# A matmul step with 96 instead of 128 weight columns, and issued one step earlier

## The chip, the cores and the metric

The kernel runs on one core of a Trainium2 chip. The metric is the device time of one execution in microseconds (us), as the median of several runs. Of the core's engines, TensorE (PE) does the matmuls, with the weight loads shown as a row of their own (PEld); VectorE (DVE) and ScalarE (ACT) do the elementwise work, SyncE (SP) issues most of the transfers.

## The reference

Three layers follow each other on 4 x 4096 = 16384 tokens of 192 channels: a causal convolution with 7 taps per head, a gated layer of 1536 hidden units, and a squared-relu layer of 2048 hidden units.

```python
out = np.einsum('hk,bskhg->bshg', w, x_unf)          # w: softmax over the 7 taps
...
gate = 1.0 / (1.0 + np.exp(-(x @ w_gate)))
val = x @ w_val
return (gate * val @ w_out).astype(np.float32)       # first layer
...
h = x @ w_in
r = np.maximum(h, 0.0)
g = r * r
return (g @ w_out).astype(np.float32)                # second layer
```

All is float32 in and out.

## The kernel before

Channels lie on partitions, tokens along the free dimension, in 32 tiles of 512 tokens. A tile goes through the gated layer (kind 1, 12 units of 128 hidden units each) and, three tiles later, through the squared-relu layer (kind 2, 8 units of 2 x 128). A unit is the work of `rows` (the matmuls into the hidden units, line 427), `activate` (ScalarE and VectorE, lines 444 to 456) and `cols` (the matmuls back to the 192 channels, line 479). PE works through them in the order in which the last loop writes them: the `rows` of a unit, then the `cols` of a unit before it.

The matmuls run on float32r operands, which hold fewer bits than float32. So each operand is split in a high and a low part, and each product is made of steps: high x high, high x low, low x high. The product of two low parts isn't needed. In `activate`, `gh` (line 455, ScalarE) is the high part of a hidden block of 128 units x 512 tokens, and `gl` (line 456, VectorE) the rest. Both have five buffers.

Every matmul uses 64 of the array's 128 rows, and each step is a pair of them, one for each half of the rows (`HALVES`). The two halves sum up in banks of their own, `sums[0]` and `sums[1]`, which `fold` adds (lines 490 to 498).

The 192 output channels make two blocks. Block a has 128 channels and the bank `accA`. Block b has 64, so its weights `wb` hold two things in their 128 columns: the 64 columns of the high part of the weights, and then the 64 columns of the low part. One step with `gh` over all 128 columns so gives high x high and low x high at once; the bank `accB` has the two on its partitions 0 to 63 and 64 to 127, and `fold` adds the one to the other (lines 497 and 498). The step with `gl` gives high x low on partitions 0 to 63, and low x low on 64 to 127.

So `cols` makes five steps (ten matmuls) for each hidden block: on accA high x gh, high x gl and low x gh, on accB all x gh and all x gl. The first step into a bank starts its sum (`start`), and the last one ends it (`stop`); start and stop are set for places 0 and 3, and 2 and 4, of the list of steps. There are 32 x 12 + 32 x 8 x 2 = 896 hidden blocks.

Weights are loaded into the array by an instruction of their own ahead of each matmul; the text of the kernel has one call for both.

Of the kernel before, what the change touches and what calls it, by code (L numbers as in the profile page):

```python
# [17 lines left out]
HB = 64  # L18
NT = 512
BLK = 32  # L20
# [4 lines left out]
def kernel(  # L25
# [356 lines left out]
    def prep_x(t, a_on_array=False, b_on_array=False):  # L382


        p, i = divmod(t, 2)
        j = p % TPB
        sa, a = convolve("A", i, lambda: xin.pop(t), j, a_on_array)
        b = []
        if i == 0:
            pairs[p], b = convolve("B", 0, lambda: xin.pop(("B", p)), j, b_on_array)  # L390

        def over():
            done(sa)
            if i == 1:
                done(pairs.pop(p))

        return a, b, part_ops(t, x1, "x1", lambda: sa["cv"], lambda: pairs[p]["cv"], over)
# [63 lines left out]
    def cols(u):  # L461

        key = (u.kind, u.t)
        if u.f == 0:
            acc[key] = [[banks.take(f"acc{nm}") for nm in "AB"] for _ in HALVES]
        sums = acc[key]
        for i, v in enumerate(u.hidden):
            if u.kind == 1:  # L470
                w, lo = w1[:, u.f, NR:], N1 + HB
            else:
                w, lo = wo2[:, 2 * u.f + i, :], NO + HB
            wa, wb, wl = w[:, 0:P], w[:, P : 2 * P], w[:, lo : lo + P]
            steps = ((0, wa, v.gh), (0, wa, v.gl), (0, wl, v.gh), (1, wb, v.gh), (1, wb, v.gl))
            first, last = u.f == 0 and i == 0, u.last and i == len(u.hidden) - 1
            for k, (b, wt, m) in enumerate(steps):
                for h, half in enumerate(HALVES):
                    nc.tensor.matmul(  # L479
                        sums[h][b][1], wt[half], m[half],  # L480
                        start=(first and k in (0, 3)), stop=(last and k in (2, 4)),
                    )
        return u.last
# [83 lines left out]
    with tc.manual_schedule():  # L567
# [59 lines left out]
        for t in range(2, NTILE):  # L627
            at = where[1, t, 0]
            before = starts[starts.index(at) - 1]
            a, b, parting = prep_x(t)  # L630
# [17 lines left out]
        for e, u in enumerate(units):  # L648
            rows(u)
            activate(u)  # L650
            for o in stores:
                o()
            stores = []
            k = e - max(s for s in starts if s <= e)
            due = len(pending) if k == 0 else 0 if k == 1 else len(pending) - 1
            for _ in range(due):
                v = pending.popleft()
                if cols(v):
                    stores += (evac1 if v.kind == 1 else evac2)(v.t)
            pending.append(u)  # L660
            for o in side[e]:
                o()
        while pending:
            v = pending.popleft()
            if cols(v):
                for o in evac2(v.t):
                    o()
# [39 lines left out]
```

## Time and profile before

| | |
|---|---|
| median of 3 runs | 2454.08 us (2453.99 to 2456.96) |
| profiled execution | 2455.46 us, its span 2453.6 us |
| PE busy | 2395.8 us (98%), 20512 matmuls |
| PEld busy | 1936.4 us (79%), 20512 loads |
| DVE busy | 1704.9 us (69%) |
| ACT busy | 1308.5 us (53%) |

The span reaches from the first to the last instruction of the profiled execution. A busy share says how much of the span an engine had something recorded as running. For PE this isn't the same as working at its peak: matmuls overlap in the array, and the profile models where they end. What can be read well is when they start.

### The profile page before, as it was taken

How to read it: one execution, taken by the hardware profiler on the slowest of the kernel's cores; microseconds unless marked ns; L12 is line 12 of the kernel's file. 1: busy time of each engine (PE TensorE's matmuls, PEld its weight loads, DVE VectorE, ACT ScalarE, POOL GpSimd, SP SyncE). 2: the span in 40 equal slices, each digit the busy share in tenths (PEclk: the TensorE clock that was granted, in tenths of full speed). 3: DMA queues.
4: the chain of work that ended last, by engine and by line, in shares of the span. 5: the costliest groups of instructions: out<-in, count | busy, mean ns of one | idle time of the engine just before them, and what ended most of it. 6: DMA issues, size and time to landing. Idle time of an engine off the chain costs nothing.

```text
span 2453.6 us, 49309 instructions
## 1 busy us (share of the span) xinstructions
PE 2395.8 (98%) x20512; PEld 1936.4 (79%) x20512; DVE 1704.9 (69%) x2676; ACT 1308.5 (53%) x2260; POOL 24.8 (1%) x97
## 2 busy tenths in 40 slices
PE   6898999999999999999999999999999999999998
PEld 3576888888888888888888888888888888888886
DVE  5776767676776766767676776766767676776676
ACT  5555555554555554555554555554555554555564
POOL 1000000000000000000000000000000000000000
PEclk8999999999999999999999999999999999999999
DMA  6232111112111121211112111121211112111111
GB/s 126 65 78 57 40 23 31 33 34 42 38 21 35 29 38 38 40 23 31 33 34 42 38 20 36 29 38 38 41 22 31 34 33 42 38 21 27 25 35 27
DMA packets 226896, 92.12 MB, mean 38 GB/s; under 512 B 202857, under 2 KB 214257, under 8 KB 226673
## 3 DMA queue, kind: packets, MB, share of 16 engines
q1 hardware_dynamic: 226272, 88.39, 17.8%
q8 instruction: 160, 2.62, 0.4%
q0 software_dynamic: 256, 0.52, 0.1%
q14 instruction: 64, 0.52, 0.1%
q10 hardware_dynamic: 144, 0.07, 0.0%
HBM read 26.03 MB, written 12.58 MB: 16 GB/s over the span
## 4 chain that ended last, share of the span: by engine, by line
PE 91%; DVE 4%; ACT 2%; issue 1%; DMA 1%; SPq 0%; DVEq 0%; ACTq 0%
PE pg L427 29%; PE accA L479 24%; PE ph L427 22%; PE accB L479 16%; DVE s L445 1%; ACT gh L455 1%; PE pv L427 1%; DVE gl L456 1%; DVE cvA L328 0%; DMA raw<-in_moe_w_out_dram 0%; ACT s L444 0%; DMA x<-x 0%; PE cv L337 0%; DVE cvB L328 0%; DVE w L168 0%
## 5 line engine op out<-in xcount | busy, mean ns | idle before, releaser
L427 PE MATMUL pg<-x,w 64*128 64x512 f32 x3456 | 866.3, 393 | 26.5 <-ACT w L157 22.4
L427 PE MATMUL pv<-x,w 64*128 64x512 f32 x3456 | 863.1, 393 | 14.2 <-DMA x<-x 10.3
L455 ACT CAST gh<-s 128x512 fp32r<-128x512 f32 x896 | 555.6, 621 | 520.0 <-DVE s L445 401.6
L456 DVE TENSOR_TENSOR gl<-s,gh 128x512 fp32r<-128x512 f32 x896 | 608.0, 692 | 286.2 <-ACT gh L455 264.0
L427 PEld LDWEIGHTS pg<-x,w 64*128 64x128 f32 x3456 | 639.3, 186 | 168.4 <-ACT w L157 27.1
L427 PEld LDWEIGHTS pv<-x,w 64*128 64x128 f32 x3456 | 639.7, 186 | 31.6 <-DVE s L445 11.6
L427 PE MATMUL ph<-x,wr 64*128 64x512 f32 x4608 | 573.4, 391 | 0.0
L427 PEld LDWEIGHTS ph<-x,wr 64*128 64x128 f32 x4608 | 431.9, 184 | 103.1 <-DVE s L445 0.4
L448 DVE TENSOR_TENSOR s<-s 128x512 f32<-128x512 f32 x512 | 330.3, 686 | 150.6 <-ACT s L447 149.7
L479 PE MATMUL accA<-gh,wo 64*128 64x512 f32 x2048 | 402.8, 390 | 0.0
L447 ACT ACTIVATE s<-ph 128x512 f32<-128x512 f32 x512 | 277.5, 594 | 214.6 <-PE ph L427 213.9
L445 DVE TENSOR_TENSOR s<-pv,s 128x512 f32<-128x512 f32 x384 | 263.2, 685 | 184.5 <-ACT s L444 184.0
L444 ACT ACTIVATE s<-pg 128x512 f32<-128x512 f32 x384 | 228.1, 594 | 245.5 <-PE pv L427 238.0
L479 PE MATMUL accA<-gh,w 64*128 64x512 f32 x1536 | 312.0, 390 | 0.0
L479 PEld LDWEIGHTS accA<-gh,wo 64*128 64x128 f32 x2048 | 192.3, 184 | 44.4
L479 PE MATMUL accA<-gl,wo 64*128 64x512 f32 x1024 | 200.4, 388 | 0.0
L479 PE MATMUL accB<-gh,wo 64*128 64x512 f32 x1024 | 200.4, 388 | 0.0
L479 PE MATMUL accB<-gl,wo 64*128 64x512 f32 x1024 | 199.9, 387 | 0.0
L479 PEld LDWEIGHTS accA<-gh,w 64*128 64x128 f32 x1536 | 157.5, 185 | 31.6 <-ACT gh L455 0.2
L479 PE MATMUL accA<-gl,w 64*128 64x512 f32 x768 | 158.5, 389 | 0.2 <-DVE gl L456 0.2
L479 PE MATMUL accB<-gh,w 64*128 64x512 f32 x768 | 158.0, 388 | 0.0
L479 PE MATMUL accB<-gl,w 64*128 64x512 f32 x768 | 157.9, 388 | 0.0
(92 smaller groups left out, 1442.4 us busy)
## 6 DMA issues: line engine op xcount, KB each, us to landing
x<-x SPq DMA_DIRECT2D x192, 256.0 KB, 3.8
out_dram<-oA SPq DMA_DIRECT2D x128, 64.0 KB, 2.0
xiA<-in_x_dram SPq DMA_DIRECT2D x124, 64.0 KB, 3.6
out_dram<-oB SPq DMA_DIRECT2D x64, 64.0 KB, 2.0
xiB<-in_x_dram SPq DMA_DIRECT2D x60, 64.0 KB, 2.8
rawr<-in_moe_w_in_dram SPq DMA_DIRECT2D x16, 192.0 KB, 3.4
rawo<-in_moe_w_out_dram SPq DMA_DIRECT2D x16, 192.0 KB, 2.5
raw<-in_moe_w_gate_dram SPq DMA_DIRECT2D x12, 192.0 KB, 3.3
```

Source lines behind the costliest of these rows:

```text
L427: nc.tensor.matmul(u.banks[h][1], w[half, o + c * P : o + (c + 1) * P], xs[1][half, place[c][h] + p, :], start=(i == 0), stop=(i == len(st ...
L444: nc.scalar.activation(s, u.banks[0][1], AF.Sigmoid)
L445: nc.vector.tensor_tensor(s, u.banks[1][1], s, op=ALU.mult)
L447: nc.scalar.activation(s, u.banks[i][1], AF.Relu)
L448: nc.vector.tensor_tensor(s, s, s, op=ALU.mult)
L455: nc.scalar.copy(v.gh, s)
L456: nc.vector.tensor_tensor(v.gl, s, v.gh.bitcast(F32), op=ALU.subtract)
L479: nc.tensor.matmul(sums[h][b][1], wt[half], m[half], start=(first and k in (0, 3)), stop=(last and k in (2, 4)),)
```

## The change

The step with gl on accB takes the first 96 (`HB + BLK`) columns of `wb` in place of all 128, and writes partitions 0 to 95 of accB. It leaves out the last 32 columns of low x low. It also changes places with the step with gh on accB, so that gl comes fourth and gh fifth. The first hidden block of each tile and layer, where accB starts its sum, keeps the old order, with gl last.

```diff
-            steps = ((0, wa, v.gh), (0, wa, v.gl), (0, wl, v.gh), (1, wb, v.gh), (1, wb, v.gl))
+
+
+            steps = [
+                (0, wa, v.gh), (0, wa, v.gl), (0, wl, v.gh), (1, wb[:, 0 : HB + BLK], v.gl), (1, wb, v.gh),
+            ]
             first, last = u.f == 0 and i == 0, u.last and i == len(u.hidden) - 1
+            if first:
+                steps[3:] = steps[:2:-1]
             for k, (b, wt, m) in enumerate(steps):
                 for h, half in enumerate(HALVES):
                     nc.tensor.matmul(
-                        sums[h][b][1], wt[half], m[half],
+                        sums[h][b][1][0 : wt.shape[1]], wt[half], m[half],
                         start=(first and k in (0, 3)), stop=(last and k in (2, 4)),
                     )
```

PE's rows for an ordinary hidden block, the second one of the first tile, stand as follows in the program before (-) and in the changed one (+); the last number is partitions x columns that a matmul writes, x2 the two halves, and `w` the weights w1.

```order
 L427 MATMUL pv<-x_179,w_70 128x512
-L479 MATMUL accA<-gh,w_70 128x512 x2
-L479 MATMUL accA<-gl,w_70 128x512 x2
-L479 MATMUL accA<-gh,w_70 128x512 x2
-L479 MATMUL accB<-gh,w_70 128x512 x2
-L479 MATMUL accB<-gl,w_70 128x512 x2
+L485 MATMUL accA<-gh,w_70 128x512 x2
+L485 MATMUL accA<-gl,w_70 128x512 x2
+L485 MATMUL accA<-gh,w_70 128x512 x2
+L485 MATMUL accB<-gl,w_70 96x512 x2
+L485 MATMUL accB<-gh,w_70 128x512 x2
 L427 MATMUL pg<-x_179,w_70 128x512
```

The two steps on accB have changed places, and the one with gl is 96 wide; 832 of the 896 blocks look like this.

At the first hidden block of the first tile, PE's rows are these.

```order
-L479 MATMUL accB<-gh,w_70 128x512 x2
-L479 MATMUL accB<-gl,w_70 128x512 x2
+L485 MATMUL accB<-gh,w_70 128x512 x2
+L485 MATMUL accB<-gl,w_70 96x512 x2
 L427 MATMUL pg<-x_179,w_70 128x512
```

Here only the width differs, as in the other 63 blocks that start a sum. No other row of PE, and no row of another engine, has moved.

## Rows read from the trace of the kernel before

**Rows 1.** The page's first part: busy time, share and instructions of PE and others.
```profile
PE 2395.8 (98%) x20512; PEld 1936.4 (79%) x20512; DVE 1704.9 (69%) x2676; ACT 1308.5 (53%) x2260; POOL 24.8 (1%) x97
```

**Rows 2.** The page's chain of work that ended last, by line.
```profile
PE pg L427 29%; PE accA L479 24%; PE ph L427 22%; PE accB L479 16%; DVE s L445 1%; ACT gh L455 1%; PE pv L427 1%; DVE gl L456 1%; DVE cvA L328 0%; DMA raw<-in_moe_w_out_dram 0%; ACT s L444 0%; DMA x<-x 0%; PE cv L337 0%; DVE cvB L328 0%; DVE w L168 0%
```

**Rows 3.** Three stretches: length, busy us (instructions) by engine, clock, DMA.
```profile
core 0: us, PE busy (x) PEld busy (x) DVE busy (x) ACT busy (x) POOL busy (x), PEclk, DMA share, GB/s
196.00:200.00 4.00, 4.00 (x22) 3.39 (x20) 1.24 (x4) 0.60 (x1) 0.19 (x1) 0.50 0.31 98
...
300.00:1300.00 1000.00, 1000.00 (x8698) 815.58 (x8696) 702.77 (x1074) 533.09 (x921) 8.14 (x35) 1.00 0.17 33
1300.00:2300.00 1000.00, 1000.00 (x8700) 815.72 (x8698) 690.75 (x1052) 527.34 (x910) 7.88 (x34) 1.00 0.17 33
```

**Rows 4.** Timeline from 1200 us: start, length (us), engine, line, instruction.
```profile
1201.07 0.39 PE L479 MATMUL accB<-gh,w 64*128 64x512 f32 x2
1201.07 0.19 PEld L479 LDWEIGHTS accB<-gl,w 64*128 64x128 f32 x2
...
1201.30 0.39 PE L479 MATMUL accB<-gl,w 64*128 64x512 f32 x2
1201.30 0.19 PEld L479 LDWEIGHTS accA<-gh,w 64*128 64x128 f32 x2
1201.52 0.39 PE L479 MATMUL accA<-gh,w 64*128 64x512 f32 x2
```

**Rows 5.** Timeline of PE from 196 us, one half's matmuls four pairs apart.
```profile
196.39 0.63 PE L427 MATMUL pv<-x,w 64*128 64x512 f32 x1
...
198.10 0.63 PE L427 MATMUL pv<-x,w 64*128 64x512 f32 x1
```

**Rows 6.** The page's costliest groups: busy us, mean ns | idle before.
```profile
L479 PE MATMUL accB<-gl,wo 64*128 64x512 f32 x1024 | 199.9, 387 | 0.0
...
L479 PE MATMUL accB<-gl,w 64*128 64x512 f32 x768 | 157.9, 388 | 0.0
```

**Rows 7.** Timeline of PEld from 31.8 us, loads of one half after a pause.
```profile
31.89 0.18 PEld L427 LDWEIGHTS pg<-x,w 64*128 64x128 f32 x1 [0.76 <-issue]
...
32.00 0.19 PEld L427 LDWEIGHTS pg<-x,w 64*128 64x128 f32 x1
```

**Rows 8.** Timeline from 167.7 us, around loads that waited for VectorE.
```profile
167.83 0.62 PE L479 MATMUL accB<-gl,w 64*128 64x512 f32 x2
...
168.06 0.39 PE L427 MATMUL pg<-x,w 64*128 64x512 f32 x1
...
168.26 0.18 PEld L427 LDWEIGHTS pv<-x,w 64*128 64x128 f32 x1 [0.25 <-DVE s L445]
...
168.29 0.47 PE L427 MATMUL pv<-x,w 64*128 64x512 f32 x1
...
168.37 0.19 PEld L427 LDWEIGHTS pv<-x,w 64*128 64x128 f32 x1
...
168.60 0.39 PE L427 MATMUL pv<-x,w 64*128 64x512 f32 x1
```

**Rows 9.** ACT's waits for line 455: us in total, times, longest us.
```profile
ACT gh L455 <- DVE s L445: 401.6, 384, 3.7
...
ACT gh L455 <- DVE s L448: 111.7, 258, 1.6
```

**Rows 10.** Timeline of PE, the last 128-row matmuls ahead of 64-row ones.
```profile
30.94 1.02 PE L337 MATMUL cv<-xTA,diag 128*128 128x512 f32 x2
...
31.37 0.59 PE L337 MATMUL cv<-xTA,diag 128*128 128x512 f32 x1
```

**Rows 11.** Timeline of PEld, two stretches: float32 loads (L337), float32r loads (L427).
```profile
8.95 0.29 PEld L337 LDWEIGHTS cv<-xTB,diag 128*128 128x128 f32 x1 [3.40 <-ACT diag L302]
...
9.11 0.34 PEld L337 LDWEIGHTS cv<-xTB,diag 128*128 128x128 f32 x1
...
60.77 0.28 PEld L427 LDWEIGHTS pg<-x,w 64*128 64x128 f32 x1 [0.95 <-DVE w L168]
...
60.94 0.33 PEld L427 LDWEIGHTS pg<-x,w 64*128 64x128 f32 x1
```

## The prediction

> **What bounds the kernel now.** I read the page's first part, then the chain of work that ended last, then the stretches. TensorE is busy for 2395.8 of 2453.6 us [rows 1], but a busy matmul engine is not yet the bound, since its ends are modelled. The chain says more: lines 427 and 479, the two loops of matmuls, hold 29 + 24 + 22 + 16 = 91% of it [rows 2]. From 300 to 2300 us the engine isn't idle for a moment, at the full clock, with 8698 and 8700 matmuls in 1000 us each [rows 3]. Matmuls run as pairs, one on each half of the array's rows, so that is 8699 pairs in 2000 us, 0.230 us each. The time of this kernel is the number of pairs times their spacing; the change keeps the number, and all depends on the spacing of the pairs that it touches.
>
> What is in a spacing? In the middle of the kernel the pairs start at 1201.07, 1201.30, 1201.52 [rows 4], each 0.23 us after the one ahead, and the weight loads of the next pair are recorded as starting together with a pair: the loads for the pair of 1201.30 begin at 1201.07 and take 0.19 us in the record. So a load runs one pair ahead, beside the pair that streams. In a stretch with the clock granted at half (1.2 GHz; 0.50 from 196 to 200 us [rows 3]) the pairs that start at 196.39 and 198.10 are four apart [rows 5], 0.4275 us each; half of that, 0.214 us, is what 512 columns would take at the full clock if nothing else counted. The real 0.230 us has 0.016 us on top. That 0.016 us is all that could be won on a pair without fewer columns of data, and whether weight loads cause it is the question.
>
> **The change, part by part.** It touches the product of the high weights of block b with the low values (gl): 1024 + 768 = 1792 matmuls with as many loads [rows 6], 896 pairs. Each keeps its 512 columns of data. It loads 96 instead of 128 weight columns per half, and writes 96 instead of 128 partitions.
>
> *The shorter load.* First, how long does a load hold up anything? After a pause the loads of a first pair start at 31.89 and those of the second pair at 32.00 [rows 7]. As the second pair's loads start when the first pair begins to stream, a load of 128 columns takes 0.11 us from start to use. Beside a spacing of 0.23 us that leaves 0.12 us of slack: one quarter off the load gives 0.03 us at most by proportion, all of it inside the slack, so 0.
>
> Second, does a load slow the pair that streams beside it? The trace has a trial of this, where loads came late because VectorE was late [rows 8]. The pair of 168.06 had streamed for 0.20 us when the loads for the next pair started at 168.26. The next matmuls are nevertheless recorded at 168.29, again 0.23 us after 168.06; they then had to wait for their weights (the loads after them start at 168.37, 0.11 us after 168.26, and the pair after that only at 168.60, 0.31 us on). I read 168.29 as the moment at which the stream of 168.06 was over, since the matmul didn't start with its load there, as it does after a pause, nor with the end of the load. So a pair without a load beside it for 0.20 of its 0.23 us was no faster. If loads cost the 0.016 us, this pair should have ended near 0.214. And the lateness fits the slack: 0.20 + 0.11 is 0.08 more than 0.23, and the pair after comes 0.31 instead of 0.23 us on. So I set the gain at 0, and keep as its other bound the whole excess: 896 x 0.016 = 14.3 us. Between them lies a share by columns, a quarter of 0.016, which gives 3.6 us. I take 0 because the late load is the nearest thing in this kernel to a load that is taken away.
>
> *The new order.* In 832 of the 896 places gl now comes ahead of gh on block b; in 64 (the first step of a tile and stage) it stays behind. No wait is added: gl was already read two steps earlier for block a, and the program has its waits where they were. Two things move by one pair. The gh buffer is read until the last step, so it comes free 0.23 us later, and gl's 0.23 us earlier. Queued behind a late gh buffer would be ScalarE's copies into gh (line 455), and behind them the low values and PE. But line 455 waits for VectorE alone in the list of waits (401.6 + 111.7 us), never for PE [rows 9]; with five buffers its cover is ample, and the price is 0. Without that cover it would be at most 896 x 0.23 = 206 us. The last step into accB stands where it stood, so line 491, which copies accB out, starts as before. No DMA and no queue but PE's is touched.
>
> *Sum.* 0 + 0. The profiled execution took 2455.46 us, 1.9 us more than its span; the changed kernel's should take the same. The median of the runs is 1.4 us lower, 2454.08, and so I forecast 2454.1 us.
>
> **The rivals.**
>
> *Loads stretch the stream after all (faster).* Then up to 0.016 us goes from each of 896 pairs: 2454.1 - 14.3 = 2439.8 us. For it speaks that there is an excess at all, and that it doesn't show at the half clock, where there is spare time to read weights. Against it stands the late load. To be seen (over 0.2%, 4.9 us, about what a measurement of this kernel can tell from no change) it must give 5.5 ns a pair, a third of the excess; a share by columns, 2450.5 us, would not be.
>
> *A change of width empties the array (slower).* All loads of the pair stream are now 128 wide; the change puts two changes of width around each of the 896 pairs. The trace has no change of width, but one of rows, from the 128-row to the 64-row matmuls: the last two of the 128-row ones start at 30.94 and 31.37, 0.43 us apart [rows 10], and the 64-row pair after them streams from 32.00 [rows 7], 0.63 us on, so 0.20 us are lost. At that price 896 x 2 x 0.20 = 358 us, 2812 us. It decides from 5.5 ns a step, 2.7 ns a change. Against it: the narrow matmuls keep their 64 rows, the same first row and the same first output partition, and what the row shows is partly a load that had not been issued ahead. The Trainium skill, "TensorEngine Tiling (Array Packing)", section "Key Properties", says that a change of the tiling mode, not of the tile alone, drains the engine. The trace agrees for the change of rows [rows 7, 10], and no run here shows whether 96 columns count as a mode.
>
> *The 128-column load is a quick form that 96 columns lose (slower).* If the load of 0.11 us became twice as long, 0.22, it would still hide under 0.23. At four times, 0.44, each of the 896 pairs would be held for 0.21 us: 188 us, 2642 us. It decides from 0.23 us plus 5.5 ns. The rows speak against a quick form: in two stretches with slow loads (0.34 and 0.33 us in the record, against 0.19 in the middle of the kernel), the first load of a plain float32 matmul of the convolution holds up the next one for 0.16 us (8.95 to 9.11), and that of a float32r matmul for 0.17 us (60.77 to 60.94) [rows 11], so the kind in use here has no lead that it could lose. This is what the Trainium skill's "TensorE: Matmul & The Clock Gate", section "Weight-path perf modes — Fast Weight Load (FWL) and DoubleRow", would bring about: it says that the quick load is used only for 128 weights of a type that isn't FP32. The trace shows no such gap between the two types.
>
> **How the numbers follow.** No change: 0.71. Loads stretch the stream by enough to be seen: 0.16. Slower: 0.13, of which a change of width 0.08, the lost quick load 0.03, a gh buffer that comes free too late 0.02. So faster 0.16, same 0.71, slower 0.13. The range begins at 2440, the whole excess gone; it ends at 2459, where slower begins, and leaves the slower cases out (0.13). The likeliest case alone would lie within 2451 to 2457, about the spread of the three runs (2453.99 to 2456.96).
>
> **What the next profile would show.** If right: the 96-column matmuls on accB have the recorded length of the others, 0.39 us, and stand 0.23 us apart from those on both sides; their loads may be recorded as shorter, by some 0.01 to 0.03 us, with nothing gained; 17,400 or so matmuls from 300 to 2300 us; line 455 still waits for VectorE only. The first rival would show spacings of 0.214 to 0.225 us at these steps and more matmuls in the same stretch. The second would show a longer spacing right before and right after each narrow pair, the third one only after loads that are recorded as far longer. My forecast is wrong if the moment 168.29 isn't the end of a stream but something set by the issue of instructions: then the late load proves only the slack, and not that loads leave the stream alone.

## The result, and the profile after

The changed kernel takes 2485.31 us (median of 4 executions, 2483.15 to 2486.22) against 2455.51 us for the kernel before beside it (2453.99 to 2456.96): a ratio of 1.012, 95% interval 1.0103 to 1.0138. It is slower by 29.8 us where no change was forecast. The profiled execution took 2483.15 us, with a span of 2481.4 us.

The page's first part for the changed kernel, as in [rows 1]:

```profile
PE 2426.0 (98%) x20512; PEld 1926.2 (78%) x20512; DVE 1706.2 (69%) x2676; ACT 1308.4 (53%) x2260; POOL 24.8 (1%) x97
```

PE is 30.2 us more busy for the same number of matmuls, its loads 10.2 us less; VectorE and ScalarE differ by 1.3 and 0.1 us. The stretches from 300 to 2300 us, with the columns of [rows 3], after the change:

```profile
300.00:1300.00 1000.00, 1000.00 (x8588) 799.93 (x8586) 692.78 (x1059) 524.64 (x906) 8.12 (x35) 1.00 0.17 33
1300.00:2300.00 1000.00, 1000.00 (x8588) 799.83 (x8586) 688.83 (x1050) 524.40 (x905) 7.86 (x34) 1.00 0.17 32
```

The clock is full and the engine is never idle, yet 1000 us hold 8588 matmuls in place of 8698 or 8700: 0.2329 us a pair, against 0.2299. Over the 10,240 pairs these 3.0 ns make 30 us, which is all of the loss. So it is a loss in the spacing of the stream, and spread over the whole of it. The timeline from 1202 us shows that no single step holds it (start, length, engine, line, instruction):

```profile
1202.04 0.39 PE L427 MATMUL pg<-x,w 64*128 64x512 f32 x1
...
1202.27 0.40 PE L485 MATMUL accA<-gh,w 64*128 64x512 f32 x2
...
1202.50 0.40 PE L485 MATMUL accA<-gl,w 64*128 64x512 f32 x2
...
1202.74 0.40 PE L485 MATMUL accA<-gh,w 64*128 64x512 f32 x2
1202.74 0.16 PEld L485 LDWEIGHTS accB<-gl,w 64*96 64x96 f32 x2
1202.97 0.40 PE L485 MATMUL accB<-gl,w 64*96 64x512 f32 x2
1202.97 0.19 PEld L485 LDWEIGHTS accB<-gh,w 64*128 64x128 f32 x2
1203.20 0.40 PE L485 MATMUL accB<-gh,w 64*128 64x512 f32 x2
...
1203.44 0.39 PE L427 MATMUL pg<-x,w 64*128 64x512 f32 x1
```

The narrow pair at 1202.97 stands 0.23 us from both neighbours, as all the others do. Its load is recorded at 0.16 us, against 0.19. From 1202.04 to 1203.44 there are six steps of 0.2333 us, and no single one sticks out. The loss is not a price paid at the narrow step.

The page's groups show it at work on a line that the change doesn't touch; the mean of the pg matmuls is 398 ns (393 before):

```profile
L427 PE MATMUL pg<-x,w 64*128 64x512 f32 x3456 | 880.4, 398 | 25.5 <-ACT w L157 21.0
```

ACT's waits for line 455 are for VectorE alone as in [rows 9], and the longer one has come down from 401.6 us:

```profile
ACT gh L455 <- DVE s L445: 393.7, 384, 3.7
```

To see spacings of this size one has to take the starts from the trace to the nanosecond. In what follows a spacing is the time from the start of one matmul to the start of the next on one half of the rows. Means from 300 to 2300 us, by kind of pair:

| ns a pair | pg and pv (line 427) | ph (line 427) | accA and accB |
|---|---|---|---|
| before | 228.9 | 233.2 | 229.2 |
| after | 233.3 | 233.4 | 232.5 |

Before, the pairs into pg and pv repeat 226, 229, 232 ns, a mean of 228.9; I call this the quick spacing. Only the pairs into ph are slower there. Their data, x2, begin at byte 139936 of each partition, which is 32 past a multiple of 64 (160 past a multiple of 512); x1 (byte 152256), gh and gl begin 192 past a multiple of 512. This holds in 30 of 32 tiles, and the others show the place at work by itself: in the last four tiles x2 stands at 139936, 152256, 139936 and 152256. The chain of work of the kernel before has a block of 36 matmuls (18 pairs) into ph early in each. Those of the second and third of these tiles:

```profile
2341.96 4.12 PE ph L427 x36
2376.78 4.19 PE ph L427 x36
```

The same line with the same weights takes 4.12 us (228.9 ns a pair) with x2 at the place of x1, in the last tile too, and 4.19 or 4.20 us (233 ns) at the other. After the change, nearly everything runs at 233, 233, 234, a mean of 233.3: the slow spacing.

### The profile page after: what moved, and what is told of

Same layout as the page of the kernel before. It is cut to its first block, busy times and chain, and to the rows that moved or that the text cites. A ratio compares the mean times of both kernels' runs of the same rounds, so it can differ in the third digit from the quotient of the medians.

```text
span 2481.4 us, 49114 instructions
## 1 busy us (share of the span) xinstructions
PE 2426.0 (98%) x20512; PEld 1926.2 (78%) x20512; DVE 1706.2 (69%) x2676; ACT 1308.4 (53%) x2260; POOL 24.8 (1%) x97
## 4 chain that ended last, share of the span: by engine, by line
PE 91%; DVE 4%; ACT 2%; issue 1%; DMA 1%; SPq 0%; DVEq 0%; ACTq 0%
PE pg L427 29%; PE accA L485 24%; PE ph L427 22%; PE accB L485 16%; DVE s L445 1%; PE pv L427 1%; ACT gh L455 1%; DVE gl L456 1%; DMA x<-x 0%; DVE cvA L328 0%; ACT s L444 0%; DMA raw<-in_moe_w_out_dram 0%; PE cv L337 0%; DVE cvB L328 0%; DVE w L168 0%
## 5 line engine op out<-in xcount | busy, mean ns | idle before, releaser
L427 PE MATMUL pg<-x,w 64*128 64x512 f32 x3456 | 880.4, 398 | 25.5 <-ACT w L157 21.0
L427 PE MATMUL pv<-x,w 64*128 64x512 f32 x3456 | 877.3, 398 | 12.4 <-DMA x<-x 9.4
L427 PEld LDWEIGHTS pg<-x,w 64*128 64x128 f32 x3456 | 644.2, 187 | 176.0 <-ACT w L157 26.0
L427 PEld LDWEIGHTS pv<-x,w 64*128 64x128 f32 x3456 | 645.1, 188 | 30.3 <-DVE s L445 10.7
L427 PE MATMUL ph<-x,wr 64*128 64x512 f32 x4608 | 574.1, 392 | 0.0
L427 PEld LDWEIGHTS ph<-x,wr 64*128 64x128 f32 x4608 | 433.2, 185 | 104.9 <-DVE s L445 0.2
L485 PE MATMUL accB<-gl,wo 64*96 64x512 f32 x1024 | 202.5, 392 | 0.0
L485 PE MATMUL accB<-gl,w 64*96 64x512 f32 x768 | 160.0, 394 | 0.0
```

The costliest lines, as they stand in the source:

```text
L427: nc.tensor.matmul(u.banks[h][1], w[half, o + c * P : o + (c + 1) * P], xs[1][half, place[c][h] + p, :], start=(i == 0), stop=(i == len(st ...
L485: nc.tensor.matmul(sums[h][b][1][0 : wt.shape[1]], wt[half], m[half], start=(first and k in (0, 3)), stop=(last and k in (2, 4)),)
```

## The experiments

Ratios are to the kernel before, run beside it on the same chip. Kernels with a narrow step leave out part of low x low, as the change does.

### One part of the change at a time

**width_alone**: 96 columns, with gh ahead of gl as before, except in the 64 blocks that end a sum (there gl stays ahead, so that the step that ends the sum writes all 128 partitions).

```diff
-            if first:
+            if not last:
                 steps[3:] = steps[:2:-1]
```

> The 96-column step stands where it stood before (last on accB), except in the 64 blocks that end a sum, where it comes ahead. Theory 'rhythm': a pair with narrow loads throws the stream of pairs from a spacing of 0.229 us into one of 0.2333 us, and the pairs behind keep it, wherever the narrow step stands: about 2485 us, with the pg and pv pairs at 0.233 us. Rival 'order': gl ahead of gh makes the loss: 2455 us. Rival 'place': each narrow step costs 33 ns at its own place: 2485 us too, but then pg and pv pairs that are far from a narrow step are at 0.229 us.

Measured: 2479.83 us, ratio 1.0092 (1.0077 to 1.0107). The pg and pv pairs stand at 233.3 ns, as theory 'rhythm' had it.

**order_alone**: gl ahead of gh, all 128 columns wide.

```diff
-                (0, wa, v.gh), (0, wa, v.gl), (0, wl, v.gh), (1, wb[:, 0 : HB + BLK], v.gl), (1, wb, v.gh),
+                (0, wa, v.gh), (0, wa, v.gl), (0, wl, v.gh), (1, wb, v.gl), (1, wb, v.gh),
```

> gl ahead of gh on accB, all loads 128 columns wide. Theory 'rhythm': no narrow load, so no change, 2455 us within 0.2%, pairs at 0.229 us with x at its aligned place. Rival 'order': 2485 us.

Measured: 2457.35 us, ratio 1.0001 (0.9992 to 1.0011). Its stretches hold the same matmuls as those of before [rows 3], 8698 and 8700; the first of them:

```profile
300.00:1300.00 1000.00, 1000.00 (x8698) 815.57 (x8696) 703.12 (x1074) 532.31 (x920) 8.19 (x35) 1.00 0.17 33
```

So the order costs nothing, and the width makes at least three quarters of the loss by itself (0.9 of 1.2%).

**one_narrow**: 96 columns only once a tile, in the third unit of the gated layer, and otherwise the order of width_alone. The new lines of the edit:

```diff
+            few = u.kind == 1 and u.f == 2
+            wn = wb[:, 0 : HB + BLK] if few else wb
```

> Only one of the 28 hidden blocks of a tile (the third of the gated layer) has a 96-column step, 32 narrow pairs in all; the order is the old one but in the 64 blocks that end a sum. Rival 'place': 32 x 33 ns = 1.1 us, 2456 us. Theory 'rhythm': the 9 gated units that follow in the tile, 14 pairs each, are slower by 4.4 ns a pair, 0.55 us a tile, 17.7 us in 32 tiles: up to 2473 us, less where something ends the slow rhythm early.

Measured: 2457.12 us, ratio 1.0001 (0.9992 to 1.0011). Theory 'rhythm' failed here as put.

**w112**: 112 columns in place of 96, otherwise the change.

> As the changed kernel, but with 112 columns. Theory 'rhythm': what matters is that the narrow load shifts the stream into another rhythm, not how much it saves, so either 2485 us like 96 columns or 2455 us like 128. Rival 'dose' (each missing column costs): half way, about 2470 us.

Measured: 2473.65 us, ratio 1.0068 (1.0053 to 1.0083). With half as many columns missing the loss is a little over half, but it isn't the same loss. The pg and pv pairs of this trace stand at 229.9 ns, nearly quick. Around a narrow pair the spacings in ns are 226 229 238 230 233 236 229 232, where the 238 lies just ahead of the narrow pair, beside its load. The four from 238 to 236 are some 20 ns longer than four quick ones, and then the quick pattern is back. 896 x 20 ns = 18 us, about the 16.5 lost. So a load of 112 columns has a price at its own place, and 'rhythm' fails again.

**w64**: 64 columns (`wb[:, 0:HB]`), which leaves out all of low x low.

> The changed kernel with 64 columns, all that block b needs; the program then gives these matmuls a tile of 64 x 64 instead of 64 x 128. If a change of tile empties the array, 0.2 us at each of two changes: 896 x 2 x 0.2 = 358 us, about 2815 us. If the tile doesn't matter: like 96 columns, 2480 to 2490 us.

Measured: 2455.8 us, ratio 0.9997 (0.9987 to 1.0007). A group of its page, and then a stretch with the columns of [rows 3]:

```profile
L485 PE MATMUL accB<-gl,wo 64*64 64x512 f32 x1024 | 200.0, 387 | 0.0
```

```profile
300.00:1300.00 1000.00, 1000.00 (x8706) 795.66 (x8704) 703.75 (x1075) 533.34 (x921) 8.18 (x35) 1.00 0.17 33
```

The tile is 64*64 between tiles of 64*128, so the shape changes twice at each of the 896 steps, and the stretch holds 8 matmuls more than before. Neither time that was expected came.

**mostly96**: all steps 96 columns wide but those that start or end a sum (8704 of 10240 pairs); it leaves out a quarter of the output columns of most products.

```diff
+            wide = P if i in (0, len(steps) - 1) else HB + BLK
...
+                full = (first and k in (0, 3)) or (last and k in (2, 4))
+                wt = wt if full else wt[:, 0 : HB + BLK]
```

> Leaves out columns 96 to 127 of most products: 8704 of the 10240 pairs are 96 wide, in runs of 7 (rows) and of 5 or 10 (cols) with 128-wide pairs between. Theory 'change of width' (it costs to go from wide to narrow and back): inside a run the spacing is 0.229 or 0.2333 us, as with 128 columns, and the loss is about 20 ns for each of some 1280 runs, 2480 to 2490 us. Rival 'narrow is slow': each narrow pair costs 18 ns, over 2600 us. Rival 'loads share with the stream': narrow pairs are quicker inside a run, 0.225 us or less, under 2440 us.

Measured: 2473.92 us, ratio 1.0071 (1.0057 to 1.0085). None of the three times that were expected came. With ten times as many narrow pairs the loss is smaller than the change's. So a 96-column load doesn't carry a fixed price.

### The place of the data

The pairs into ph are slow in the kernel before, and their data stand 32 bytes off. Would the kernel gain if they stood straight? The halo tiles that lie ahead of x are widened, which moves x1, x2, gh and gl. No work changes.

```diff
-                h = halo[nm, seqs] = xp.tile([P, PAD], F32, tag=f"ha{nm}{seqs}", name="ha" + nm)
+                wide = PAD if (nm, seqs) == ("A", 0) else PAD + 4
+                h = xp.tile([P, wide], F32, tag=f"ha{nm}{seqs}", name="ha" + nm)[:, 0:PAD]
+                halo[nm, seqs] = h
```

**aligned_before** (the kernel before with this edit: x2 at 139968, x1 at 152320) and **aligned_after** (the changed kernel with it).

> The kernel before, with both places of the x tiles at a multiple of 64 bytes (one stood 32 bytes off). In the trace of before the pairs that read the one off are 0.2333 us apart, all others 0.229. Theory 'rhythm' (the stream has a quick and a slow rhythm, and the place of the moving data decides between them there): the 2304 ph pairs gain 4.3 ns each, 9.9 us, ratio 0.996. Rival: ph pairs are slower for another reason (their weights, the work beside them): ratio 1.000.

> The changed kernel with both places of the x tiles at a multiple of 64 bytes. Theory 'rhythm': the slow rhythm comes from the narrow step, not from the place of x; with nothing to end it, nearly all pairs stay at 0.2333 us: as slow as the changed kernel or some us slower, ratio 1.012 to 1.014. Rival 'place of x': the slow rhythm enters through the x tile that is off and the narrow step only carries it on: the stream goes back to 0.229 and only the narrow steps cost, 16 us or less less 10 for ph: ratio 1.000 to 1.003.

Measured: 2472.95 us, ratio 1.0067 (1.0053 to 1.008), and 2473.3 us, 1.0067 (1.0055 to 1.008). Neither expectation held in either run. In aligned_before the pairs into ph became quick, 229.7 ns, but those into pg and pv slow, 233.1 ns. And at these places the narrow step costs nothing in sum: in aligned_after the accA and accB pairs are 1.0 ns slower (232.7), those into pg and pv 0.9 ns quicker (232.2).

**x_at_64** and **x_at_64_after** (widths 16 and 32 for the two halo tiles, x at 139968 and 152384), and **x_at_64_w64** (the same places, 64 columns).

> The kernel before with both places of the x tiles at 64 bytes past a multiple of 128, where one of them, gh and gl already stand; weights as before at a multiple of 128. Theory 'places' (a pair's spacing depends on where the moving data lies modulo 128 bytes beside the loads that are read at the same time: 64 is the quick place, 0 and 32 are slow): the 2304 ph pairs go from 0.2333 to 0.229 us, 9.9 us less, ratio 0.996, no other pair changes. Rival: places don't matter and the run with x at multiples of 64 was slow for another reason: ratio 1.000 or above.

> The same places, with the 96-column step. Theory 'places and lengths' (a 96-column load breaks the quick pattern, and only the x tile 32 bytes off ended the slow one): slow rhythm nearly everywhere, ratio 1.012 or above. Rival: with all data at the quick place each narrow step costs only its own 18 to 23 ns: 2457 + 16 to 21 - 10 us, ratio 1.003 to 1.005.

> x at the quick place and the gl step on block b with 64 columns and a 64 x 64 tile. With 64 columns and the old places the loss was nil; so as with the x places alone, ratio 0.996; if the 64-column step costs something that was hidden, 0.998 to 1.004.

Measured: 1.0082 (1.0068 to 1.0096), 1.005 (1.0038 to 1.0063) and 1.01 (1.0086 to 1.0114). Here the step with 96 columns made the kernel faster (2469.43 us against 2477.74 with 128), and the one with 64 columns didn't (2482.47). The theories' times came in none of the three. That 1.005 lies within the rival's range for x_at_64_after is a chance hit: the rival counted on a gain of 10 us from the places, and x_at_64 lost 20.

**weights_at_64**: the weights 64 bytes on, everything else 128, by two unused tiles.

> The kernel before with all weights moved to 64 past a multiple of 128, data unchanged (x at 32 and 64, gh and gl at 64). If what counts is the place of the data relative to that of the weights, gh, gl and one x tile are now at distance 0, as in the run with x at multiples of 64, whose pairs were 0.2317 us apart: about 2475 us, ratio 1.007. If the place of the data alone counts: 1.000.

Measured: 2490.08 us, ratio 1.0134 (1.0118 to 1.0149), with not one narrow load; its pairs into pg, pv, accA and accB alternate between some 238 and 229 ns. Neither expectation held. The run doesn't show what the weights' place does: x1, gh and gl stand at the same bytes as in x_at_64 (x1 at 152384), and the pg and pv pairs are as slow there, 233.6 ns against 233.3. The ph pairs, at 233.8 ns against 229.3, had x2 at another place, 140064.

The gain expected of straighter data came in none of these. What they show is that the places in memory alone move the spacing, anywhere from that of before to worse than that of after, and that the effect of the narrow step depends on them. By kind of pair, in these traces without a narrow load and in that of before, data that begin 192 past a multiple of 512 went with means of 228.9 to 229.7 ns, and data at 160, 256, 288 or 320 with 231.7 to 233.8.

### Where in the pattern the narrow load falls

one_narrow had shown no loss, though the change loses on far more pairs than it touches. In the quick spacing 226, 229 and 232 take turns, so a narrow load meets one of the three. The unit in which it stands chooses which: a unit of the gated layer is 14 pairs (9 of `rows`, 5 of `cols`), two more than a multiple of three.

**narrow_f1** and **narrow_f3**: as one_narrow, with `u.f == 1` and `u.f == 3`.

> Only one 96-column step a tile, 32 in all, as in the run with one narrow step, but at the second hidden block of the gated layer instead of the third. Before, the pairs repeat a pattern of three spacings, 0.226, 0.229 and 0.232 us; at the third block the narrow loads fall beside a pair of 0.229 and cost 23 ns in all, at the second one they fall beside a pair of 0.232. Theory 'phase': in the changed kernel narrow loads beside a pair of 0.232 threw the stream into the slow rhythm, so here the 112 pairs that follow until the second layer's turn are 4.4 ns slower each: 0.5 us a tile, 14 to 16 us, about 2473 us, ratio 1.006. Rival 'place': 32 x 33 ns, 1 us, ratio 1.000.

> The same with the fourth hidden block, where the narrow loads fall beside a pair of 0.226 us. Theory 'phase': in the run with the old order such a narrow step left no trace, so nothing here: ratio 1.000, and the pairs around it keep 0.226, 0.229, 0.232. Rival 'each narrow step can start it': like the second block, ratio 1.006.

Measured: narrow_f1 2472.44 us, 1.0063 (1.0049 to 1.0077); narrow_f3 2457.43 us, 0.9999 (0.999 to 1.0008). The same 32 narrow steps, and 15 us between them. Spacings in ns around a narrow pair in the three kernels (n stands behind the spacing that follows the narrow pair; its load runs beside the spacing ahead of that):

```
narrow_f1   232 225 230 233 232n 233 233 234 233 233 234 233 233 234 233 233
one_narrow  229 232 225 236 232n 237 231 232 226 229 232 225 230 231 226 229
narrow_f3   226 229 232 225 230n 231 226 229 232 226 229 232 225 230 231 226
```

Beside what would have been a 232 (narrow_f1) the pattern is gone, and stays gone. Beside a 229 (one_narrow) the five spacings from 236 on are some 20 ns longer in all, and the pattern returns. Beside a 226 (narrow_f3) nothing happens. How long it stays gone shows in the timeline of narrow_f1, from the narrow pair to the last pair ahead of the next ph block:

```profile
885.16 0.40 PE L487 MATMUL accB<-gl,w 64*96 64x512 f32 x2
...
911.29 0.40 PE L487 MATMUL accB<-gl,w 64*128 64x512 f32 x2
911.52 2.26 PE L427 MATMUL ph<-x,wr 64*128 64x512 f32 x18
```

and, the same 112 steps, in that of narrow_f3:

```profile
878.87 0.39 PE L487 MATMUL accB<-gl,w 64*128 64x512 f32 x2
...
904.50 0.39 PE L487 MATMUL accB<-gl,w 64*128 64x512 f32 x2
904.73 0.39 PE L427 MATMUL ph<-x,wr 64*128 64x512 f32 x2
```

26.13 against 25.63 us: 0.2333 and 0.2288 us a pair. The first 112 hold one narrow load, at their start; the 111 pairs behind it are 128 wide and still slow. This stretch is slow in 28 of the 32 tiles of narrow_f1, and in none of narrow_f3. 28 x 0.50 = 14 us, nearly all of the 15.4. So theory 'phase' held in both runs. It holds for 96 columns: in w112 the narrow load too meets what would have been a 232, and the pattern returns four pairs on.

**x_at_192** and **x_at_192_after**: widths 16 and 128, which puts x2 too at 192 past a multiple of 512 and leaves x1, gh and gl at such places.

> The kernel before with both places of the x tiles, and gh and gl as before, at 192 past a multiple of 512 bytes (one x place stood at 160, the rest at 192). So far each pair that read data at 192 beside 128-column loads was 0.229 us from the next, at 0, 64 and 160 it was 0.231 to 0.234. Theory 'places': the 2304 ph pairs gain 4.3 ns each, 9.9 us, ratio 0.996, nothing else changes. Rival: other pairs get slow as in the two runs with moved x: ratio 1.006 or above.

> The same places with the 96-column step. Theory 'phase': once a narrow step falls beside a pair of 0.232 us the slow rhythm starts, and here no pair with data elsewhere ends it: 0.2333 us nearly everywhere, ratio 1.012 to 1.016. Rival: ratio 1.005 or less.

Measured: x_at_192 2446.88 us as the median of five executions, 0.9957 (0.9943 to 0.997) by four of them; x_at_192_after 2489.22 us, 1.0132 (1.0117 to 1.0148). Both theories' times came. The same change now costs 1.8% (1.0132 / 0.9957) and not 1.2%. The stretches of x_at_192_after, 8574 matmuls in each, hold 0.2333 us a pair throughout; the first of them:

```profile
300.00:1300.00 1000.00, 1000.00 (x8574) 802.28 (x8572) 691.61 (x1056) 522.96 (x903) 7.82 (x35) 1.00 0.17 33
```

Four executions of x_at_192 took 2444.93 to 2448.42 us. The fifth, the only one with a trace, took 2489.24 us and isn't in the ratio. From 300 to 2300 us all its pairs stand at 233.3 ns, the slow spacing, without a narrow load. And the two halves are out of step:

```profile
299.71 0.39 PE L481 MATMUL accA<-gh,w 64*128 64x512 f32 x1
...
300.41 0.39 PE L481 MATMUL accB<-gh,w 64*128 64x512 f32 x1
300.44 0.39 PE L481 MATMUL accA<-gh,w 64*128 64x512 f32 x1
```

The other half's first accA<-gh comes at 300.44, 0.73 us or three pairs behind the one of 299.71. The trace shows how this came about. At 247.24 us, behind a wait, the two halves start the same step within 1 ns, and from there their spacings in ns are

```
one half    231 226 229 232 226 229 232 225
the other   234 233 233 234 233 233 234 233
```

They drift apart by 4.4 ns a pair, until from about 285 us on both are slow. So each half has a spacing of its own, and the slow one can begin without a narrow load; what began it here isn't known. In the traces of before, after and x_at_192_after the halves start within 5 ns of each other from 350 us on.

**x_at_192_gl_off**: x_at_192 with one of the five gl buffers 32 bytes off.

```diff
-            v.gl = gp.tile([P, NT], F32R, tag="gl", name="gl", bufs=5)
+            turn = glturn[0] = (glturn[0] + 1) % 5
+            off = 8 if turn == 4 else 0
+            v.gl = gp.tile([P, NT + off], F32R, tag=f"gl{turn}", name="gl", bufs=1)[:, off:]
```

> No narrow load. The places are those of the run x_at_192 (all data of the 128-wide pairs at 192 bytes past a multiple of 512), but one of the five buffers of gl starts 32 bytes off, as x2 does in the kernel before. Theory (a pair whose data starts 32 bytes off ends the slow rhythm of 0.2333 us a pair, and the quick one, 0.2289, starts behind it): two pairs in ten of cols with that buffer are some 4 to 5 ns slower themselves, 2 x 896 / 5 = 358 pairs or 1.6 us, but no execution stays in the slow rhythm: all are at 0.995 to 0.998 of the kernel before, and none is near 2487 us. Rival (the pairs that are 32 bytes off end nothing, and x_at_192 only happened to start quick): some executions near 2487 us as before. Second rival (such a pair sets the stream off in either rhythm, by its place): a time between, 2455 to 2485 us, in all executions, with stretches at 0.2333.

Measured: 2450.23 us over 9 executions (2447.94 to 2455.12), 0.9972 (0.9962 to 0.9981). None was near 2487 us. But x_at_192 itself had only one such execution in five, and in that one the halves were out of step besides, so nine without one don't decide what was asked.

**narrow_f1_gl_off**: narrow_f1 with the same edit to gl.

> As narrow_f1 (one 96-column step in the second unit of each tile's gated layer; it leaves out 32 columns of low x low there; places of the kernel before), but one of the five buffers of gl starts 32 bytes off. narrow_f1 lost 15 us, as the 112 pairs between its narrow step and the next block of ph pairs, whose data start 32 bytes off, ran at 0.2333 us each: 32 x 112 x 4.3 ns. Theory (a pair with data 32 bytes off ends the slow rhythm): now it lasts only to the next use of that buffer, one to five units of 11 pairs on, 33 pairs in the mean: 32 x 33 x 4.3 ns = 4.5 us, and some 1.6 us for the slower pairs with that buffer; ratio 1.0015 to 1.0035, and the trace shows pairs 0.2333 apart only from the narrow step to that buffer's next use. Rival (these pairs end nothing; the ph block ends it by something else): the stretch to the ph block stays slow, ratio 1.006 to 1.007.

Measured: 2467.64 us, ratio 1.0046 (1.0033 to 1.006), between the two expectations. In its trace neither holds as put. Two tiles, the spacings around the narrow pair (o: behind a pair with data 32 bytes off):

```
narrow at 585.8 us  229 232 225 230 233 232n 233 233 234 ... 233 234 238o 230 232 238o 230 232 233 233 234
narrow at 438.4 us  232 226 229 231 226 229n 232 226 229 232 226 229 231 226 229 232 226
```

In the first the narrow load meets a 232, and the slow spacing goes on past the pairs that are 32 bytes off: 238, 230 and 232 make three times 233.3. It lasts to the ph block. So a single such pair ends nothing, and my theory fell there. (Its unit of 11 pairs is 14; with that it would have given 7.4 us, ratio 1.003.) In the second the pattern reached the narrow load shifted, so that it met a 226, and nothing was lost. This is the case in some tiles, and in others the narrow pair itself read the buffer that is off; 17 of 32 tiles still turn slow, against 28 in narrow_f1. 17 x 0.50 us, and the 1.6 us of the slower pairs, make 10.1 of the 10.6 us lost.

## Why the prediction was wrong

**The bound: right.** PE's stream sets the time, and all depended on the spacing of its pairs: 3.0 ns a pair on 10,240 pairs is the whole loss.

**"How long does a load hold up anything": right.** The narrow load is recorded 0.03 us shorter and gains nothing. The signs that the prediction gave for being right nearly all came, 0.23 us on both sides of the narrow pair among them; at 0.01 us they couldn't show a loss of 3 ns a pair, and only the count of matmuls did, 17,176 in place of 17,400.

**"Does a load slow the pair that streams beside it": the step that failed.** It read the late load as a trial of a load taken away, and priced a narrower load at 0 for the stream on both sides. The late load shows what it was said to show, one pair that was 0.23 us long without a load beside it [rows 8]. But it was read at 10 ns, and the question was one of 4 ns: behind two more late loads of that trace, at 181.98 and 214.70 us, the matmuls of the two halves follow after 234, 234, 225 and 236 ns, which spreads wider than the 226 to 232 of the undisturbed stream. More than that, it looked for the effect on one pair, at the load. The effect is on the pairs behind: a 96-column load that meets a 232 pair turns the stream from 0.2289 to 0.2333 us for over a hundred 128-wide pairs (narrow_f1). With 896 narrow loads in 10,240 pairs it stays there most of the time, and the term that stood at 0 measured 29.8 us. In the trace of the changed kernel a ph block of the second layer is followed by 225, 229, 233, the last of them beside the first narrow load, and then by 231 to 235 up to the next ph block. The mean spacing of 0.230 us [rows 3] was in fact a mix of 228.9 and 233.2, and I took it for one number with an unknown excess. Whether 168.29 is the end of a stream, which the prediction named as its weak point, wasn't tried; the loss doesn't turn on it.

**"The new order ... the price is 0": right** by itself (order_alone 1.0001). With the narrow load it may matter a little, as it decides where the load falls: width_alone is at 1.0092, the change at 1.012. Behind a ph block the first narrow load of width_alone falls beside a 226 and leaves no trace, and only the second one, five pairs on, meets a 232; in the change the first one does.

**A change of width empties the array: wrong mechanism, right side.** In the changed kernel the spacings ahead of and behind the narrow pair have means of 234.4 and 231.6 ns, 233 on the whole, so no price stands there. In w112 one does, but of 20 ns a step and not of 400. With w64 the shape of the tile itself changes at each of the 896 steps, and the ratio is 0.9997. The Trainium skill's "TensorEngine Tiling (Array Packing)", section "Key Properties", has a drain for a change of mode, not for one of tile; by these runs 64*128 to 64*64 with the same rows isn't such a change, or costs nothing.

**The lost quick load: wrong.** The narrow load is recorded as shorter, not longer, and mostly96, with 8704 of 10240 pairs narrow, loses less than the change.

**Loads stretch the stream (faster): not this way.** With w64 the accA and accB pairs go from 229.2 to 228.9 ns; 0.3 ns is all that a load of half the columns gave back.

What the loss hangs on, then, is shown: the width of the narrow step, the place in the pattern where its load falls (narrow_f1, one_narrow, narrow_f3), and the places in memory. That it is the load and not the narrower write to the bank is argued: every run narrowed both, and what speaks for the load is that the first spacing to change is the one ahead of the narrow matmul (236 for 229 in one_narrow). Why 112 columns cost 20 ns and 64 nothing is open. What ends the slow spacing is only partly settled. In the kernel before and in narrow_f1 the quick one returns behind a ph block whose data are 32 bytes off (225, 229, 232 follow it); in x_at_192_after, with ph data at 192, ph blocks end nothing; one pair that is 32 bytes off ends nothing either. A whole block of them is what is left. The last four tiles of the changed kernel bear it out: the accA and accB pairs of the second layer have means of 231.7 and 231.9 ns in the two tiles with x2 at 139936, and 233.3 in the two with x2 at 152256. It was not tried by a run of its own. Why the array has two spacings isn't known from these runs.

## What to carry to other kernels

Where a stream of matmuls is the bound, its spacing is a term of its own: take it to the nanosecond, by kind of pair, before pricing an edit at 0 because it hides in slack. A change of load width, or of where a buffer stands, can move that spacing for pairs that the edit doesn't touch, in either direction, so such an edit is tried and not argued. Moving x2 by 32 bytes and x1 by 512 gave 0.43% with no change of work in four of five executions, and the fifth was 1.3% slower than before.

## What the runs showed of the hardware that was not expected

- The same 128-wide pairs run at 0.2289 or at 0.2333 us each, for over a hundred pairs on end, by what happened ahead of them. The Trainium skill's "TensorE: Matmul & The Clock Gate", section "Back-to-back issue gap", gives fixed figures for 512 columns, about 216 ns for an isolated matmul and about 131 ns a matmul in a sustained stream. Neither fits here: on each half, no kind of 128-wide pair had a mean under 228.9 ns, and two halves at work make 114 ns a matmul.
- The start of the data in a partition moves the spacing by up to 4 ns: 32 bytes on x2 take the ph pairs from 233.2 to 229.2 ns (x_at_192_gl_off, where x1, gh and gl moved by 512), and in the kernel before the same block takes 4.20 or 4.12 us by the place of x2.
- The two halves of the array can run at different spacings at the same time, and fall out of step by three pairs and stay so: one execution of x_at_192, at 2489 us where its others took 2445 to 2448. Matmuls of the two halves then start out of the program's order: accB<-gh of one half at 300.41, ahead of the other's accA<-gh at 300.44.
